# Layer-1 PV of four KV heads with V stationary, and the output projection of two of them with its weights stationary

## The chip, the cores and the metric

The kernel runs on one core of a Trainium2 chip. The metric is the device time of one execution in microseconds. Medians below are of all runs; where the fast runs alone give another size, both are given.

## The reference

One decode step of eight batch rows goes through two layers, each an attention over a cached window of 1024 positions and a feed-forward block:

```python
def _A_ref(x, k_cache, v_cache, wq, wo):       # 16 query heads, 8 KV heads (kvh), Dh = 256
    q = (x @ wq) ...
    k, v = the last W = 1024 positions, each kvh used by two query heads
    p = softmax(q k^T * Dh ** -0.5)
    return (p v) @ wo
x = x + _A_ref(_layernorm(x), k, v, wq, wo)     # layer 1, attention
x = x + _B_ref(_layernorm(x), w1, w2)           # silu feed-forward, D = 448, F = 1792
x = x + _A_ref(_layernorm(x), k, v, wq, wo)     # layer 2: the same caches and weights
x = x + _B_ref(_layernorm(x), w1, w2)
```

TensorE (PE in the profiles) does a matmul by holding one operand in its array (it is *stationary*) and streaming the columns of the other through (they *move*). PV is the product of the softmax weights p with V, wo the output projection.

Each batch row brings 8 K and 8 V tiles of 512 KB, 8.39 MB; together with the weights 77.7 MB are loaded. Both layers use the same tiles, so a tile stays in its slot until layer 2 has used it.

## The kernel before

A planner takes tasks with estimated durations and priorities, puts them in one static order per engine and inserts the semaphores. The table BIAS shifts the priorities; it was tuned for this list of tasks. PE's instructions run in that order and no other.

```python
def pv_rows(b, layer, k2, prio, oT_dst, oT_key, nj=4):   # p stationary (2 columns), V moves (256 columns)
    ...   # four KV heads side by side in four column groups of the array
    fns.append(lambda e, ...: e.matmul(bank[ob][32 * j:32 * j + 2, c0:c0 + DH], pt, vv, ...,
                                       tile_position=(0, 32 * j)))
    # then: ACT evicts the rows, two matmuls transpose them, DVE scales them into oT1

def pv_cols(b, layer, kvh, prio, oT_dst, oT_key):        # V stationary (128 columns), p moves (2 columns)
    for a in range(2):
        for u in range(8):
            fns.append(lambda e, ...: e.matmul(bank[vb][:, c0 + 2 * a:c0 + 2 * a + 2],
                                               vs[:, ...128 columns of V...], pT_sb[ei][:, u, 2 * kvh:2 * kvh + 2], ...))
    # then: DVE scales the columns into oT1, no transpose

def wo_part(b, kvhs, last, prio):                        # o stationary (1 column), wo moves (449 columns)
    ...   # 4 matmuls per kvh, accumulated as rows in bank XB

def fold(prio, scale, reads):                            # rows of XB -> columns of x in bank YB
    act(... rowb <- bank[XB] ...)                        # eviction, 0.55 us
    keep(2, prio, "part")                                # filler: 512-wide products with zero weights, results unused
    to_cols(YB, 0, rowb, ones4, 1, ...)                  # 6 matmuls: 3 of 128 columns, 2 of 64, 1 of 128

# layer 1 of batch b (cut)
pv_rows(b, 0, 0, prio, oT1, "oT1")                       # kvh 0-3
if b > 0:
    idle(4, prio, "s1", XB)                              # filler
wo_part(b, (0, 1), 7, prio + 1)
wo_part(b, (2, 3), 7, prio + 1)
pv_rows(b, 0, 1, prio, oT1, "oT1", 3)                    # kvh 4, 5, 6
wo_part(b, (4, 5, 6), 7, prio)
pv_cols(b, 0, 7, prio, oT1, "oT1")                       # kvh 7
wo_part(b, (7,), 7, prio)
fold(prio, 1.0, [])
# then layer 2 of b: feed-forward, q, scores (which free the K slots), softmax, PV (which frees the V slots)
```

Of the kernel before, what the change touches and what calls it, by code (L numbers as in the profile page):

```python
# [7 lines left out]
ALU = mybir.AluOpType  # L8
# [17 lines left out]
HOLD, PE_SCALE = 0.503, 1.091  # L26
BIAS = {"dve.KT.0.a": 11.7, "dve.KT.1.a": -6.0, "pe.S0.0.a": 9.3, "dve.mT.0.a": -6.1, "dve.mg.0.a": 26.6,
        "pe.pT.0.a": 16.5, "dve.eT.0.a": -27.1, "pe.l.0.a": 2.8, "dve.lsum.0.a": 22.2, "pe.S0.1.a": 30.5,
        "pe.pT.1.a": 11.2, "act.rsum.a": -40.4, "act..a": 25.9, "pe.PV0.0.0.a": 23.2, "pe.PV0.0.1.a": 1.7,
        "pe.PV0.0.2.a": 6.9, "pe.PV0.0.3.a": 48.5, "pe.oT.a": 7.8, "dve.oTev.a": 17.4, "pe.wo.a": 8.1,  # L30
        "pe.PV0.1.0.a": 82.1, "pe.PV0.1.1.a": 52.7, "pe.PV0.1.2.a": 74.5, "pe.PV0.1.3.a": 51.0, "pe.PVc.a":
        12.3, "pe.keep.a": 27.9, "pe.fold.a": 30.9, "dve.xb.b": 6.6, "pe.stat.b": 27.0, "pe.w1.b": 12.2,
        "pe.keep.b": -10.7, "pe.w2.b": 33.9, "pe.fold.b": 26.1, "pe.wq.b": 9.5, "pe.qturn.b": 12.2, "dve.qT2.b":
        53.5, "pe.qsel.b": 37.8, "pe.S1.0.b": 11.8, "dve.max.b": 15.5, "pe.S1.1.b": 14.2, "pe.l.c": 13.4,
        "pe.PV1.0.0.c": 11.3, "pe.PV1.0.1.c": 46.9, "pe.PV1.0.2.c": 10.7, "pe.PV1.0.3.c": 35.0, "pe.oT.c": 8.5,
        "pe.idle.a": 3.8, "pe.idle.b": 41.7}
# [220 lines left out]
def bass_interleave_layers__sliding_block_cached__dense_activation_silu__decode_kernel(  # L257
# [9 lines left out]
    P = 128  # L267
# [8 lines left out]
    XC = 5  # L276
# [73 lines left out]
    def bk(i):  # L350
        return [("bank", i)]
# [343 lines left out]
    def pv_rows(b, layer, k2, prio, oT_dst, oT_key, nj=4):  # L695
# [4 lines left out]
        for q in range(4):  # L700
            fns = []
            for u in (2 * q, 2 * q + 1):
                for j in range(nj):
                    vv = slots[slot_of[b, "v", 4 * k2 + j]][:, u * DH:u * DH + DH]
                    pt = pT_sb[ei][:, u, 8 * k2 + 2 * j:8 * k2 + 2 * j + 2]
                    fns.append(lambda e, u=u, j=j, vv=vv, pt=pt: e.matmul(  # L706
                        bank[ob][32 * j:32 * j + 2, c0:c0 + DH], pt, vv, start=(u == 0), stop=(u == 7),
                        tile_position=(0, 32 * j), skip_group_check=True))
            vr = range(4 * k2, 4 * k2 + nj)
            pe(fns, [("slot", slot_of[b, "v", g]) for g in vr] + [("pT", ei, k2)], bk(ob), (DH, 4), prio,  # L710
               "PV%d.%d.%d.%d" % (layer, b, k2, q))
# [7 lines left out]
            oT_dst[:, :, k2 * 8:k2 * 8 + 2 * nj],  # L719
            bank[lb][:, C_O + k2 * 16:C_O + k2 * 16 + 16].rearrange("p (a n) -> p a n", a=2)[:, :, 0:2 * nj],  # L720
            rl_sb[ei][:, k2 * 8:k2 * 8 + 2 * nj].unsqueeze(1).broadcast_to([P, 2, 2 * nj]), ALU.mult),
            bk(lb) + [("rl", ei, k2)], [(oT_key, 2 * h) for h in range(4 * k2, 4 * k2 + nj)], 0.18, prio, "oTev")

    def pv_cols(b, layer, kvh, prio, oT_dst, oT_key):

        ei, k2, j = layer, kvh // 4, kvh % 4
        vs = slots[slot_of[b, "v", kvh]]
        vb = LB[layer]
        c0 = C_Q + 4 * j
        fns = []  # L730
        for a in range(2):
            for u in range(8):
                fns.append(lambda e, a=a, u=u: e.matmul(
                    bank[vb][:, c0 + 2 * a:c0 + 2 * a + 2], vs[:, u * DH + a * P:u * DH + (a + 1) * P],
                    pT_sb[ei][:, u, 2 * kvh:2 * kvh + 2], start=(u == 0), stop=(u == 7)))
        pe(fns, [("slot", slot_of[b, "v", kvh]), ("pT", ei, k2)], bk(vb), (2, 1), prio, "PVc.%d" % b)
        dve(lambda e: e.tensor_tensor(
            oT_dst[:, :, 2 * kvh:2 * kvh + 2], bank[vb][:, c0:c0 + 4].rearrange("p (a n) -> p a n", a=2),
            rl_sb[ei][:, 2 * kvh:2 * kvh + 2].unsqueeze(1).broadcast_to([P, 2, 2]), ALU.mult),
            bk(vb) + [("rl", ei, k2)], [(oT_key, 2 * kvh)], 0.18, prio, "oTev")  # L740
# [23 lines left out]
    def wo_part(b, kvhs, last, prio):  # L764
# [8 lines left out]
        pe(fns, [("oT1", 2 * kvh) for kvh in kvhs] + WO_R, bk(XB) + ["part"], (D, 4), prio, "wo")  # L773
# [14 lines left out]
    def fold(prio, scale, reads):  # L788

        act(lambda e: e.activation(rowb, bank[XB][:, 0:D1], ACTF.Copy, scale=scale), bk(XB) + reads, ["rowb"], 0.6,  # L790
            prio, "rowb")
        keep(2, prio, "part")
        to_cols(YB, 0, rowb, ones4, 1, prio, ["rowb"] + ONES4, "fold", (120, 1))

    def chain(b, prio):
# [13 lines left out]
        fold(prio, rhalf[:, 0:1], ["rhalf"])  # L809
# [134 lines left out]
    def layer1(b):  # L944
# [17 lines left out]
        if b > 0:  # L962
            idle(4, prio, "s1", XB)
        wo_part(b, (0, 1), 7, prio + 1)
        wo_part(b, (2, 3), 7, prio + 1)
        pv_rows(b, 0, 1, prio, oT1, "oT1", 3)
        wo_part(b, (4, 5, 6), 7, prio)
        pv_cols(b, 0, 7, prio, oT1, "oT1")
        wo_part(b, (7,), 7, prio)
        fold(prio, 1.0, [])  # L970
# [57 lines left out]
```

## Time and profile before

| | before |
|---|---|
| time, median of 3 | 246.25 us (245.55 to 248.67) |
| PE busy | 192.4 of 247.1 us |
| DVE busy | 167.3 us |
| end of loading | about 210 us |
| mean granted clock | 0.993 |

The page cuts the span into 40 slices. In the PE row a digit is the busy share in tenths; PEclk is the granted TensorE clock in tenths of full speed, and GB/s is what the loads moved.

In the timeline, the reference mark for it is the group of 16 w1 matmuls of 448 columns, four side by side:

```profile
150.16 0.93 PE L522 MATMUL bank<-w_sb,xbt 128*1 128x448 bf16 x16
```

In the timeline, the columns are start, duration, engine, line, operation with output and inputs, and the count.

### The profile page before, as it was taken

The page shows a single profiled execution, that of the slowest core. Times are in us where ns is not written, and L with a number is a line of the kernel's source. Part 1 is how long each engine was busy: PE and PEld are TensorE (multiplying, and loading weights), DVE is VectorE, ACT ScalarE, POOL GpSimd, SP SyncE. Part 2 cuts the span into 40 slices and gives each one's busy share as a digit, 9 for nine tenths or more (in the row PEclk, how much of TensorE's full clock was granted, in tenths as well). Part 3 has the DMA queues.
Part 4 walks back from the last instruction along what each step waited for, and adds up shares of the span by engine and source line. Part 5 has one row for each costly group of instructions (what it writes and reads, how often), then busy time and mean ns, then how long its engine had stood idle before and what let it go on. Part 6 is the DMA issues. An engine that isn't in the chain of part 4 may idle for free.

```text
span 247.1 us, 8606 instructions
## 1 busy us (share of the span) xinstructions
PE 192.4 (78%) x3780; PEld 101.5 (41%) x3780; DVE 167.3 (68%) x485; ACT 89.1 (36%) x249; POOL 11.8 (5%) x25
## 2 busy tenths in 40 slices
PE   0050430379779999999999979979899999998796
PEld 0050210133345446555544645445455545444453
DVE  6549774955975888689588858956795888322322
ACT  2001172754323443253344325432534352333212
POOL 1200000000000000000000000000000000000000
PEclk9999999999999999999999999999999999999989
DMA  6999999999999998999999999999989998000000
GB/s 228 365 359 396 289 340 379 411 362 381 406 407 413 406 408 313 397 411 379 377 411 409 312 396 395 380 326 389 359 324 378 406 409 325 8 3 0 3 3 1
DMA packets 25652, 78.22 MB, mean 317 GB/s; under 512 B 2304, under 2 KB 8336, under 8 KB 25232
## 3 DMA queue, kind: packets, MB, share of 16 engines
q1 hardware_dynamic: 25616, 77.68, 83.8%
q8 instruction: 29, 0.48, 0.8%
q14 instruction: 7, 0.06, 0.1%
HBM read 77.67 MB, written 0.01 MB: 314 GB/s over the span
## 4 chain that ended last, share of the span: by engine, by line
PE 54%; SPq 21%; DMA 12%; DVE 5%; ACT 5%; issue 3%; ACTq 0%
PE bank L706 11%; DMA slot<-in_A_k_cache_dram 9%; PE bank L644 9%; SPq L485 6%; PE bank L818 6%; SPq L480 5%; SPq L442 5%; PE bank L770 4%; PE bank L777 4%; PE bank L522 2%; PE bank L805 2%; DMA slot<-in_A_v_cache_dram 2%; PE bank L784 2%; ACT qbd L676 2%; PE bank L681 2%
## 5 line engine op out<-in xcount | busy, mean ns | idle before, releaser
L953 DVE STREAM_TRANSPOSE slot<-slot 128x512 uint32<-128x512 uint32 x128 | 83.2, 686 | 7.6 <-DMA slot<-in_A_k_cache_dram 7.3
L706 PE MATMUL bank<-slot,pT_sb 128*2 128x256 bf16 x960 | 40.6, 285 | 16.3 <-DMA slot<-in_A_v_cache_dram 13.1
L644 PE MATMUL bank<-slot,qbd 128*8 128x256 bf16 x1024 | 39.2, 284 | 4.7 <-DVE slot L953 2.6
L706 PEld LDWEIGHTS bank<-slot,pT_sb 128*2 128x2 bf16 x960 | 21.5, 85 | 26.1 <-issue 19.1
L644 PEld LDWEIGHTS bank<-slot,qbd 128*8 128x8 bf16 x1024 | 22.0, 86 | 11.9 <-DVE slot L953 3.1
L676 ACT ACTIVATE qbd<-bank,mseg 128x256 bf16<-128x256 f32 x32 | 14.3, 473 | 23.1 <-DVE mseg L672 12.5
L712 ACT ACTIVATE qbd<-bank 128x256 bf16<-128x256 f32 x32 | 12.2, 382 | 24.2 <-PE bank L706 23.8
L755 POOL TENSOR_TENSOR cols_f<-cols_f 128x1 f32<-128x1 f32 x16 | 8.8, 552 | 205.3 <-ACT cols_f L753 205.3
L613 ACT ACTIVATE qbd<-bank,cols_f 128x128 bf16<-128x128 f32 x32 | 12.0, 375 | 18.2 <-PE bank L608 17.6
L777 PE MATMUL bank<-wq_sb,cols_b 128*128 128x512 bf16 x64 | 18.1, 381 | 0.0
L770 PE MATMUL bank<-wo_sb,oT 128*1 128x449 bf16 x256 | 17.8, 377 | 0.2
L718 DVE TENSOR_TENSOR oT<-bank,l_sb 128x16 bf16<-128x16 f32 (+1 forms) x32 | 6.4, 199 | 16.3 <-PE bank L714 15.7
L818 PE MATMUL bank<-wq_sb,xbt 128*1 128x512 bf16 x256 | 16.5, 378 | 0.3 <-DVE xbt L744 0.3
L784 PE MATMUL bank<-wq_sb,cols_b 128*128 128x512 bf16 x49 | 14.7, 382 | 0.0
L825 ACT ACTIVATE qrow<-bank 128x512 bf16<-128x512 f32 x16 | 9.6, 597 | 13.1 <-PE bank L818 13.1
L681 PE MATMUL bank<-qbd,swap 128*128 128x256 bf16 x32 | 7.8, 283 | 6.5 <-ACT qbd L676 6.1
L685 ACT ACTIVATE pT_sb<-bank 128x64 bf16<-128x64 f32 (+1 forms) x24 | 5.8, 241 | 19.1 <-DVE bank L684 19.1
L684 DVE STREAM_TRANSPOSE bank<-bank 128x256 f32<-128x256 f32 x24 | 10.8, 451 | 2.6 <-PE bank L681 1.4
L461 DVE TENSOR_REDUCE qbd<-wo_sb 128x5 f32<-128x2240 bf16 x4 | 9.7, 2478 | 3.6 <-DMA wo_sb<-in_A_wo_dram 3.6
L744 DVE SCALAR_TENSOR_TENSOR xbt<-bank,mask 128x5 bf16<-128x5 f32 x16 | 3.6, 226 | 9.9 <-PE bank L545 9.7
L689 DVE TENSOR_REDUCE l_sb<-bank 128x8 f32<-128x64 f32 (+1 forms) x24 | 5.7, 237 | 6.4 <-PE bank L687 6.4
L515 PE MATMUL bank<-qbd,wq_sb 128*128 128x16 bf16 x128 | 3.6, 174 | 6.9 <-DMA wq_sb<-in_A_wq_dram 6.9
(151 smaller groups left out, 237.4 us busy)
## 6 DMA issues: line engine op xcount, KB each, us to landing
slot<-in_A_k_cache_dram SPq DMA_DIRECT2D x64, 512.0 KB, 8.4
slot<-in_A_v_cache_dram SPq DMA_DIRECT2D x64, 512.0 KB, 8.2
wo_sb<-in_A_wo_dram SPq DMA_DIRECT2D x1, 3584.0 KB, 17.8
wq_sb<-in_A_wq_dram SPq DMA_DIRECT2D x3, 1024.0 KB, 6.9
w_sb<-in_B_w_dram SPq DMA_DIRECT2D x4, 336.0 KB, 16.1
w_sb<-in_B_w_dram SPq DMA_DIRECT2D x1, 1344.0 KB, 16.4
wq_sb<-in_A_wq_dram SPq DMA_DIRECT2D x2, 256.0 KB, 10.6
w_sb<-in_B_w_dram SPq DMA_DIRECT2D x4, 112.0 KB, 12.0
```

Source lines behind the costliest of these rows:

```text
L442: dma(lambda e, j=j: e.dma_start(rows[:, 3 * j:3 * j + 3, :], parts[j, 0:3 * P, :].rearrange("(c p) n -> p c n", p=P)), [("w2", j)], 3 * P ...
L480: dma(lambda e: e.dma_start(slots[s][:, :].rearrange("p (u d) -> p u d", d=DH), A_k_cache[b, kvh, S0:SK, :].rearrange("(p u) d -> p u d", ...
L485: dma(lambda e: e.dma_start(slots[s][:, :], A_v_cache[b, kvh, S0:SK, :].rearrange("(p u) d -> p (u d)", p=P)), [("slot", s)], W * DH * 2, ...
L644: fns.append(lambda e, cb=cb, par=par, j=j, kvh=kvh, kv=kv: e.matmul(bank[sc][32 * j:32 * j + 8, k2 * 256:(k2 + 1) * 256], qbd[qi][:, kvh, ...
L676: act(lambda e, k2=k2: e.activation(e_sb[ei][:, k2, :], bank[sc][:, k2 * 256:(k2 + 1) * 256], ACTF.Exp, bias=mb[ei][:, k2:k2 + 1], scale=1.0),
L681: pe([lambda e, k2=k2: e.matmul(t, swap[:, 8 - 8 * k2:8 - 8 * k2 + P], e_sb[ei][:, k2, :], start=(k2 == ks[0]), stop=(k2 == ks[-1])) for k ...
L706: fns.append(lambda e, u=u, j=j, vv=vv, pt=pt: e.matmul(bank[ob][32 * j:32 * j + 2, c0:c0 + DH], pt, vv, start=(u == 0), stop=(u == 7), ti ...
L770: fns.append(lambda e, i=i, c=c, kvh=kvh: e.matmul(bank[XB][32 * c:32 * c + 1, 0:D1], oT1[:, i % 2, i // 2:i // 2 + 1], wo_sb[:, i * DP:i ...
L777: pe([lambda e: e.matmul(bank[SC[1]][:], zero_b.broadcast_to([P, P]), wq_sb[:, 0:512], start=False, stop=True, skip_group_check=True) for ...
L784: pe(lambda e: e.matmul(bank[bi][:], zero_b.broadcast_to([P, P]), wq_sb[:, 0:512], start=False, stop=True, skip_group_check=True), [("wq", ...
L818: pe([lambda e, j=j, c=c, k2=k2, wb=wb: e.matmul(bank[wb][32 * j:32 * j + 1, :], xbt[:, xcol(c, k2):xcol(c, k2) + 1], wq_sb[:, c * HD + (( ...
L953: dve(lambda e, v=v: e.transpose(v, v), [("slot", s)], [("slot", s)], 0.67, prio, "KT.%d.%d" % (b, k // 4))
```

## The change

The layer-1 work after the last load of a batch was to become shorter. With V stationary, each KV head can be worked on alone as soon as its load has landed and the softmax of its half is done. With the wo weights stationary, the result of kvh 6 and 7 lands in the columns of x at once, so the eviction and the fold of the wo rows need not wait for them. The filler matmuls beside that fold go, and idle goes in batches 2 to 6. BIAS was tuned again.

```diff
-        if b > 0:
+        if b == 1 or b == NB - 1:
             idle(4, prio, "s1", XB)
-        wo_part(b, (0, 1), 7, prio + 1)
-        wo_part(b, (2, 3), 7, prio + 1)
-        pv_rows(b, 0, 1, prio, oT1, "oT1", 3)
-        wo_part(b, (4, 5, 6), 7, prio)
-        pv_cols(b, 0, 7, prio, oT1, "oT1")
-        wo_part(b, (7,), 7, prio)
-        fold(prio, 1.0, [])
+        wo_part(b, (0, 1), 5, prio + 1)
+        wo_part(b, (2, 3), 5, prio + 1)
+        pv_cols(b, (4, 5), LB[0], prio)
+        wo_part(b, (4, 5), 5, prio)
+        fold(prio, 1.0, [], 0)
+        pv_cols(b, (6,), OB[0], prio)
+        wo_cols(b, 6, prio)
+        pv_cols(b, (7,), LB[0], prio)
+        wo_cols(b, 7, prio)
...
+    def wo_cols(b, kvh, prio):
+        fns = []
+        for i in range(4 * kvh, 4 * kvh + 4):
+            o = oT1[:, i % 2, i // 2:i // 2 + 1]
+            for c in range(XC):                       # 3 pieces of 128 columns, 2 of 64
+                fns.append(lambda e, i=i, c=c, o=o: e.matmul(
+                    bank[YB][xpart(c), c:c + 1], xpiece(wo_sb[:, i * DP:i * DP + D], c), o, start=False, stop=True,
+                    tile_position=xpos(c), skip_group_check=True))
+            fns.append(lambda e, i=i, o=o: e.matmul(
+                bank[YB][:, XC:XC + 1], wo_sb[:, i * DP + D:i * DP + D1].broadcast_to([P, P]), o, start=False, stop=True,
+                skip_group_check=True))
...
-        keep(2, prio, "part")
+        if n:
+            keep(n, prio, "part")
```

More of the change, by code (lines that the diff above doesn't have):

```diff
@@ L25 @@
 SP_ISSUE, DMA_FIRST, DMA_LAST = 0.47, 1.2, 2.2
-HOLD, PE_SCALE = 0.503, 1.091
-BIAS = {"dve.KT.0.a": 11.7, "dve.KT.1.a": -6.0, "pe.S0.0.a": 9.3, "dve.mT.0.a": -6.1, "dve.mg.0.a": 26.6,
-        "pe.pT.0.a": 16.5, "dve.eT.0.a": -27.1, "pe.l.0.a": 2.8, "dve.lsum.0.a": 22.2, "pe.S0.1.a": 30.5,
-        "pe.pT.1.a": 11.2, "act.rsum.a": -40.4, "act..a": 25.9, "pe.PV0.0.0.a": 23.2, "pe.PV0.0.1.a": 1.7,
-        "pe.PV0.0.2.a": 6.9, "pe.PV0.0.3.a": 48.5, "pe.oT.a": 7.8, "dve.oTev.a": 17.4, "pe.wo.a": 8.1,
-        "pe.PV0.1.0.a": 82.1, "pe.PV0.1.1.a": 52.7, "pe.PV0.1.2.a": 74.5, "pe.PV0.1.3.a": 51.0, "pe.PVc.a":
-        12.3, "pe.keep.a": 27.9, "pe.fold.a": 30.9, "dve.xb.b": 6.6, "pe.stat.b": 27.0, "pe.w1.b": 12.2,
-        "pe.keep.b": -10.7, "pe.w2.b": 33.9, "pe.fold.b": 26.1, "pe.wq.b": 9.5, "pe.qturn.b": 12.2, "dve.qT2.b":
-        53.5, "pe.qsel.b": 37.8, "pe.S1.0.b": 11.8, "dve.max.b": 15.5, "pe.S1.1.b": 14.2, "pe.l.c": 13.4,
-        "pe.PV1.0.0.c": 11.3, "pe.PV1.0.1.c": 46.9, "pe.PV1.0.2.c": 10.7, "pe.PV1.0.3.c": 35.0, "pe.oT.c": 8.5,
-        "pe.idle.a": 3.8, "pe.idle.b": 41.7}
+HOLD, PE_SCALE = 0.503, 1.094
+BIAS = {"dve.KT.0.a": 22.1, "dve.KT.1.a": -3.9, "pe.pT.0.a": 6.7, "dve.eT.0.a": -25.5, "pe.S0.1.a": 7.7,
+        "pe.xinit.a": -3.8, "dve..a": 14.1, "act.rsum.a": 44.5, "pe.PV0.0.0.a": 33.7, "pe.PV0.0.2.a": -46.3,
+        "pe.PV0.0.3.a": -28.4, "act.oev.a": 45.6, "pe.wo.2.a": 44.7, "pe.wo.4.a": 39.0, "pe.fold.a": 15.8,
+        "pe.PVc.6.a": 19.1, "dve.oTev.6.a": -2.3, "pe.woc.6.a": 11.5, "pe.PVc.7.a": 15.7, "pe.woc.7.a": 14.3,
+        "dve.xb.b": 20.2, "pe.stat.b": 50.4, "pe.keep.b": -1.5, "pe.w2.b": 48.6, "act.qrow.b": 40.5,
+        "pe.qturn.b": 1.0, "pe.qsel.b": 21.7, "pe.S1.0.b": 0.2, "dve.max.b": -4.5, "pe.S1.1.b": -27.9,
+        "dve.mT.c": 18.4, "pe.pT.c": 10.4, "pe.l.c": 2.1, "dve.rl.c": -6.4, "pe.PV1.0.0.c": -1.1,
+        "pe.PV1.0.1.c": 43.4, "pe.oT.c": 24.5, "dve.oTev.c": -6.6, "pe.PV1.1.0.c": -1.9, "pe.xinit8.c": 12.6,
+        "pe.idle.e": -7.1, "dve.xbt8.e": 22.2}
 class Task:
@@ L693, in softmax, with pv_rows @@
             [(x, ei, k2) for k2 in ks for x in ("l", "rl")], 0.25 if part is None else 0.2, prio, "rl" + tag)
-    def pv_rows(b, layer, k2, prio, oT_dst, oT_key, nj=4):
+    def pv_rows(b, layer, k2, prio, oT_dst, oT_key):
         ob, lb, ei = OB[layer] if b < NB - 1 or k2 == 0 else OB[0], LB[layer], layer
@@ L702, in pv_rows @@
             for u in (2 * q, 2 * q + 1):
-                for j in range(nj):
+                for j in range(4):
                     vv = slots[slot_of[b, "v", 4 * k2 + j]][:, u * DH:u * DH + DH]
@@ L708, in pv_rows @@
                         tile_position=(0, 32 * j), skip_group_check=True))
-            vr = range(4 * k2, 4 * k2 + nj)
+            vr = range(4 * k2, 4 * k2 + 4)
             pe(fns, [("slot", slot_of[b, "v", g]) for g in vr] + [("pT", ei, k2)], bk(ob), (DH, 4), prio,
@@ L718, in pv_rows @@
         dve(lambda e: e.tensor_tensor(
-            oT_dst[:, :, k2 * 8:k2 * 8 + 2 * nj],
-            bank[lb][:, C_O + k2 * 16:C_O + k2 * 16 + 16].rearrange("p (a n) -> p a n", a=2)[:, :, 0:2 * nj],
-            rl_sb[ei][:, k2 * 8:k2 * 8 + 2 * nj].unsqueeze(1).broadcast_to([P, 2, 2 * nj]), ALU.mult),
-            bk(lb) + [("rl", ei, k2)], [(oT_key, 2 * h) for h in range(4 * k2, 4 * k2 + nj)], 0.18, prio, "oTev")
-    def pv_cols(b, layer, kvh, prio, oT_dst, oT_key):
-        ei, k2, j = layer, kvh // 4, kvh % 4
-        vs = slots[slot_of[b, "v", kvh]]
-        vb = LB[layer]
-        c0 = C_Q + 4 * j
-        fns = []
-        for a in range(2):
-            for u in range(8):
-                fns.append(lambda e, a=a, u=u: e.matmul(
-                    bank[vb][:, c0 + 2 * a:c0 + 2 * a + 2], vs[:, u * DH + a * P:u * DH + (a + 1) * P],
-                    pT_sb[ei][:, u, 2 * kvh:2 * kvh + 2], start=(u == 0), stop=(u == 7)))
-        pe(fns, [("slot", slot_of[b, "v", kvh]), ("pT", ei, k2)], bk(vb), (2, 1), prio, "PVc.%d" % b)
-        dve(lambda e: e.tensor_tensor(
-            oT_dst[:, :, 2 * kvh:2 * kvh + 2], bank[vb][:, c0:c0 + 4].rearrange("p (a n) -> p a n", a=2),
-            rl_sb[ei][:, 2 * kvh:2 * kvh + 2].unsqueeze(1).broadcast_to([P, 2, 2]), ALU.mult),
-            bk(vb) + [("rl", ei, k2)], [(oT_key, 2 * kvh)], 0.18, prio, "oTev")
@@ new lines, in pv_rows, with pv_cols @@
+            oT_dst[:, :, k2 * 8:k2 * 8 + 8],
+            bank[lb][:, C_O + k2 * 16:C_O + k2 * 16 + 16].rearrange("p (a n) -> p a n", a=2)[:, :, 0:8],
+            rl_sb[ei][:, k2 * 8:k2 * 8 + 8].unsqueeze(1).broadcast_to([P, 2, 8]), ALU.mult),
+            bk(lb) + [("rl", ei, k2)], [(oT_key, 2 * h) for h in range(4 * k2, 4 * k2 + 4)], 0.18, prio, "oTev")
+    def pv_cols(b, kvhs, vb, prio):
+        n, h0 = 2 * len(kvhs), 2 * kvhs[0]
+        c0 = C_Q + 4 * (kvhs[0] - 4)
+        for kvh in kvhs:
+            vs = slots[slot_of[b, "v", kvh]]
+            fns = []
+            for a in range(2):
+                cc = c0 + n * a + 2 * kvh - h0
+                for u in range(8):
+                    fns.append(lambda e, a=a, u=u, cc=cc, vs=vs, kvh=kvh: e.matmul(
+                        bank[vb][:, cc:cc + 2], vs[:, u * DH + a * P:u * DH + (a + 1) * P],
+                        pT_sb[0][:, u, 2 * kvh:2 * kvh + 2], start=(u == 0), stop=(u == 7)))
+            pe(fns, [("slot", slot_of[b, "v", kvh]), ("pT", 0, 1)], bk(vb), (2, 1), prio, "PVc.%d.%d" % (b, kvh))
+        dve(lambda e: e.tensor_tensor(
+            oT1[:, :, h0:h0 + n], bank[vb][:, c0:c0 + 2 * n].rearrange("p (a n) -> p a n", a=2),
+            rl_sb[0][:, h0:h0 + n].unsqueeze(1).broadcast_to([P, 2, n]), ALU.mult),
+            bk(vb) + [("rl", 0, 1)], [("oT1", 2 * kvh) for kvh in kvhs], 0.18, prio, "oTev.%d.%d" % (b, kvhs[0]))
@@ new lines, in wo_cols @@
+    def wo_cols(b, kvh, prio):
+        fns = []
+        for i in range(4 * kvh, 4 * kvh + 4):
[7 more added lines that the diff above has]
+                skip_group_check=True))
+        pe(fns, [("oT1", 2 * kvh)] + WO_R, bk(YB), (1, 1), prio, "woc.%d.%d" % (b, kvh))
@@ L772, in wo_part @@
                     start=(kvh == 0), stop=(kvh == last), tile_position=(0, 32 * c), skip_group_check=True))
-        pe(fns, [("oT1", 2 * kvh) for kvh in kvhs] + WO_R, bk(XB) + ["part"], (D, 4), prio, "wo")
+        pe(fns, [("oT1", 2 * kvh) for kvh in kvhs] + WO_R, bk(XB) + ["part"], (D, 4), prio, "wo.%d.%d" % (b, kvhs[0]))
     def keep(n, prio, after):
@@ L786, in idle, with fold @@
                [("wq", 0), "zero_b", after], bk(bi), (512, 1), prio, "idle")
-    def fold(prio, scale, reads):
+    def fold(prio, scale, reads, n):
         act(lambda e: e.activation(rowb, bank[XB][:, 0:D1], ACTF.Copy, scale=scale), bk(XB) + reads, ["rowb"], 0.6,
             prio, "rowb")
-        keep(2, prio, "part")
+        if n:
+            keep(n, prio, "part")
         to_cols(YB, 0, rowb, ones4, 1, prio, ["rowb"] + ONES4, "fold", (120, 1))
@@ L808, in chain @@
             for f in range(FC)], ["hT"] + W2_R, bk(XB) + ["part"], (D, 4), prio, "w2")
-        fold(prio, rhalf[:, 0:1], ["rhalf"])
+        fold(prio, rhalf[:, 0:1], ["rhalf"], 2)
         xcols(prio)
```

## The prediction

> **What bounds the kernel now.** I read the page first, then the queue's waits, the chain of waits and the timeline of PE over four batches. The page shows three resources close to full at once:
>
> ```profile
> PE 192.4 (78%) x3780; PEld 101.5 (41%) x3780; DVE 167.3 (68%) x485; ACT 89.1 (36%) x249; POOL 11.8 (5%) x25
> ...
> PE   0050430379779999999999979979899999998796
> ...
> GB/s 228 365 359 396 289 340 379 411 362 381 406 407 413 406 408 313 397 411 379 377 411 409 312 396 395 380 326 389 359 324 378 406 409 325 8 3 0 3 3 1
> ```
>
> Loading ends in slice 34 (34 x 247.1/40 = 210 us). Until then the rate touches 410 GB/s but falls to 312-326 about once per batch; the last 37 us are one latency chain without loads. From slice 12 on PE is "busy" nearly always, but filler matmuls (the lines named keep and idle, on zeros) are part of that.
>
> Why the dips: the load queue waits for slots. In its own waits:
>
> ```profile
> SPq L485 <- PE bank L828: 49.8, 7, 9.6
> ```
>
> That is the load of V6 of the next batch, waiting 7 us in each batch for PE to pass the layer-2 scores of the first four heads of this one (they stand just before L828 in program order). There are 30 slots and 16 tiles per batch, so V6 and V7 of batch b+1 take slots of K0-3 of batch b. Hence a **loop**: layer-2 scores of b end -> V6, V7 of b+1 are issued and land -> layer-1 PV, wo, fold -> FFN, q -> layer-2 scores of b+1. The chain shows it once outright:
>
> ```profile
> 160.14 5.84 DMA slot<-in_A_v_cache_dram
> 165.98 0.25 issue
> 166.23 1.04 PE bank L706 x24
> ```
>
> The 24 matmuls are the layer-1 PV rows of kvh 4, 5 and 6. What then lies between V6 and the end of fold, in the timeline of PE:
>
> ```profile
> 166.23 1.04 PE L706 MATMUL bank<-slot,pT_sb 128*2 128x256 bf16 x24 [1.21 <-DMA slot<-in_A_v_cache_dram]
> 167.20 0.21 PE L714 MATMUL bank<-ident,qbd 128*128 128x8 bf16 x2
> 167.27 0.38 PE L681 MATMUL bank<-qbd,swap 128*128 128x256 bf16 x2
> 167.68 0.55 PE L770 MATMUL bank<-wo_sb,oT 128*1 128x449 bf16 x8
> 168.16 0.21 PE L714 MATMUL bank<-ident,qbd 128*128 128x8 bf16 x2
> 168.30 0.55 PE L770 MATMUL bank<-wo_sb,oT 128*1 128x449 bf16 x8
> 168.78 0.56 PE L733 MATMUL bank<-pT_sb,slot 128*128 128x2 bf16 x16
> 169.27 1.04 PE L706 MATMUL bank<-slot,pT_sb 128*2 128x256 bf16 x32
> 170.14 0.93 PE L770 MATMUL bank<-wo_sb,oT 128*1 128x449 bf16 x16
> 171.00 0.60 PE L777 MATMUL bank<-wq_sb,cols_b 128*128 128x512 bf16 x2
> 171.44 0.22 PE L687 MATMUL bank<-pT_sb,cols_b 128*128 128x128 bf16 x1
> ```
>
> Fold starts at 171.91 and ends about 172.3, 6.1 us after the V6 work began. The loop in numbers: scores end 160.04; V6 in use 166.23 (6.2); fold done 172.3 (6.1); next scores end 183.62 (11.3). Sum 23.6, as measured. In the batches without that DMA wait V6 is used 4.9 us after the scores, still with little to spare. The starts of the L733 group, one per batch, lie at 122.54, 144.48, 168.78, 191.07 and 213.28: periods of 21.94, 24.30, 22.29 and 22.21, mean 22.7. The load alone would need 8.39 MB / 410 GB/s = 20.5.
>
> **What the Trainium skill says.** "TensorE: Matmul & The Clock Gate", the section on the 56 ns gap, gives a floor of about 25 ns from start to start for small matmuls. The trace agrees: 16 PV columns (L733) take 0.49 us and 4 of L828 take 0.19, so (0.49-0.19)/12 = 25 ns each plus about 0.09 on entering. "TensorEngine Tiling (Array Packing)", Key Properties, says that changing the tiling mode drains TensorE. The trace agrees: fold has three 128-wide matmuls, two 64-wide, one 128-wide:
>
> ```profile
> 154.80 0.35 PE L542 MATMUL bank<-cols_b,qrow 128*128 128x1 bf16 x5
> 155.08 0.18 PE L545 MATMUL bank<-cols_b,qrow 128*128 128x1 bf16 x1
> 155.19 0.41 PE L644 MATMUL bank<-slot,qbd 128*8 128x256 bf16 x8
> ```
>
> In narrow windows the 64-wide pair starts at 154.96, so three, two and one matmuls take 0.16, 0.12 and 0.11 us, where 25 ns each would make 0.08, 0.05 and 0.03. Each switch costs about 0.08 us. "DMA: Bandwidth & Descriptors" (Anatomy of one DMA) puts about 2 us of fixed time on a load. The trace agrees roughly: V6 takes 5.84 us, of which its own 0.52 MB at 410 GB/s are 1.3; for a us after 160 only 156 GB/s move. The first page's part on clock oscillation explains the fillers (idle PE lets its clock fall); the granted clock is 1.00 in all four periods, so the trace does not show what fewer of them do.
>
> **The change part by part**, per batch.
>
> (1) The PV rows of kvh 4-6 go: 24 matmuls, 0.76 us (163.59 to 164.35 without a wait), their ACT eviction (0.38) and their two L714 matmuls (0.14). Three column groups of 16 come: 3 x 0.49 = 1.47. They can start as soon as V4, V5 have landed, before V6 is there. PE: +0.57.
>
> (2) wo of kvh 6 and 7: 8 row matmuls go, 8 x 0.048 = 0.38 (L770 starts 0.76-0.86 apart for 16). In come 2 x 24 matmuls with weights stationary. Each of the 8 rows i is the fold pattern of 3 + 2 + 1 with two mode switches: about 0.31 us by the fold's 0.16 + 0.12 and one joining on at 25-30 ns, so 4 x 0.31 = 1.2 per kvh and 2.4 in all. Without the switches it would be 48 x 0.025 + 0.2 = 1.4. PE: +2.0.
>
> (3) rowb (ACT 0.55) and fold (PE 0.39) remain but cover kvh 0-5 only and move ahead of V6's landing, off the loop. The two keep matmuls beside them go (0.44), and in batches 2 to 6 four idle ones (4 x 0.22 = 0.88). PE: -1.32.
>
> Net on PE: +0.57 + 2.0 - 1.32 = **+1.25 us per batch** in batches 2 to 6, +2.1 in batches 1 and 7, where idle stays.
>
> On the loop: from V6, the new way is PVc.6 0.49, woc.6 1.2, PVc.7 0.49, its eviction about 0.3, woc.7 1.2 and x about 0.25: 3.9 us. V7's path alone (1.3 later, then 2.2) is shorter. So 6.1 becomes 3.9 and the loop of 23.6 would be 21.4; with V6 after 4.9 it would be 20.1, about the load's own 20.5. The loop stops binding, by up to **2.2 us per batch**.
>
> But PE's in-order stream then binds. Of the undisturbed period of 21.94 I work out some 1.0 us as waits (0.76 shown as not busy, and short ones hidden in the modelled ends of matmuls). 21.94 + 1.25 - 1.0 = 22.2 is the floor by PE if every wait is filled; the work that stood between V6 and fold (the layer-2 PV of the batch before, a softmax, wo of kvh 0-3) does not vanish, it only has to stand elsewhere. Against the mean of 22.7 that is 0.5 saved on some five periods, 2.3 us. The last batch has nothing left to overlap with: there PE's +2.1 is partly on the path, and rowb and fold (about 1.0 with their handovers) come off it: +1.0. Sum: 246.25 - 2.3 + 1.0 = **245.0 us**.
>
> **The rivals.** (a) *The loop is what counts and the extra PE work drops into waits*: period 21.2, (22.7-21.2) x 6 = 9 us less, 237 to 240. For it: the dips, the 49.8 us of queue waits, the fillers as evidence that the author had PE time to spare. Against it: PE has only 5.5 us of shown idle time from 90 to 215 us. (b) *PE becomes the bound*: no wait can be filled, the period rises to 21.94 + 1.25 or so, 23.2, and the end moves to 249 to 251. For it: PE was already at 21.2 to 21.3 busy in every period; the mode switches, which the kernel's own planner (0.0265 us per small matmul) doesn't know, so that its order is made with woc 0.5 us too short. Against it: keep and idle are real slack that was put into the stream where waits were expected. (c) *The loads were hidden anyway*: the end is set by the last batch's chain, and only its +1 or -1 us shows. Against it: the last chain cannot start before loading and the periods have passed. (d) Stalls named "issue" (1.30 at 145.90, 0.71 at 174.13), which no dependency explains: some 56 more matmuls per batch may bring more of them.
>
> **Range and chances.** Between (a) and (b) the sign is open. I put a quarter on (a), rather less on (b), the rest between: 245.0, range 240 to 250.5. Faster by over 2% means under 241.3, slower means above 251.2. Faster 0.27, same 0.57, slower 0.16. I add a little weight to faster, because the fillers were retuned for the new order.
>
> **What would show each step.** Group L733's successor with 64 matmuls per batch at 25-30 ns: step 1. The woc groups from start to the next start: 1.2 us each means that the mode switches bite, 0.7 that they don't, and then PE is 1.0 us per batch lighter and (a) gains. The queue's wait for the layer-2 scores: well below 49.8 us, with the dips gone, if the loop is shortened; unchanged if PE took its place. The distance between column groups of successive batches: 22.2, against 21.2 for (a) and 23.2 for (b). From V6's landing to the x column: 3.9. Idle time of PE outside the fillers: near none. The prediction is wrong if woc is far from 1.2, if the order puts other PE work between V7 and x again, or if the granted clock falls where fillers were dropped.

## More of the kernel before

A run counts as "fast" when it lies within 1.5% of the fastest run of its kernel.

The clock row of the kernel before is the one that the prediction did not show:

```profile
PEclk9999999999999999999999999999999999999989
```

The clock stays at the top all the time, apart from one slice near the end.

## The result

| | before | changed |
|---|---|---|
| median | 247.46 us (4 runs, 245.55 to 252.44) | 272.0 us (4 runs, 271.19 to 273.07) |
| granted clock of the runs | 0.98 to 1.00 (the runs of before beside the experiments) | 0.906 to 0.937 |

The ratio is 1.102 (95% interval 1.092 to 1.113): 10% slower. A ratio here is the mean time of one kernel's fast runs over that of the other's of the same rounds, so it is not quite the ratio of the medians quoted.

The page of the changed kernel, the rows of the slices:

```profile
PE 210.0 (78%) x4215; PEld 123.0 (46%) x4240; DVE 170.9 (63%) x493; ACT 86.0 (32%) x241; POOL 11.8 (4%) x25
...
PEclk9999999999997999599959997998699889979999
...
GB/s 246 348 408 367 312 356 409 384 370 408 353 369 272 331 364 381 261 324 327 380 217 369 290 401 255 373 344 352 232 365 345 310 290 341 160 2 2 0 2 4
```

Two things are new. The clock falls once per batch, in some slices to half. And the dips of the load rate, which the change was to remove, are deeper: 217 to 272 GB/s where before they reached 312 to 326. The load queue's waits for slots have not gone, they have moved and grown: from 98 us in all to 119. The two longest (the first, in front of the K loads, was 28.9 us before):

```profile
SPq L479 <- PE bank L764: 50.2, 6, 9.2
...
SPq L484 <- PE bank L843: 38.1, 6, 11.5
```

What stands between the softmax and the x column of one batch, in the timeline of PE (L733 is PV by columns, L784 wo by rows, L705 layer 2's PV by rows, L541 and L544 the fold, L748 and L751 the new wo columns, L764 the first use of x, L521 w1):

```profile
154.93 0.20 PE L686 MATMUL bank<-pT_sb,cols_b 128*128 128x64 bf16 x1 [0.60 <-ACT pT_sb L684]
154.96 0.55 PE L733 MATMUL bank<-pT_sb,slot 128*128 128x2 bf16 x16
...
156.47 0.95 PE L733 MATMUL bank<-pT_sb,slot 128*128 128x2 bf16 x32 [0.26 <-DVE oT L717]
157.35 1.31 PE L784 MATMUL bank<-wo_sb,oT 128*1 128x449 bf16 x24
158.59 0.56 PE L733 MATMUL bank<-pT_sb,slot 128*128 128x2 bf16 x16
159.08 0.61 PE L705 MATMUL bank<-slot,pT_sb 128*2 128x256 bf16 x16
159.62 0.35 PE L541 MATMUL bank<-cols_b,qrow 128*128 128x1 bf16 x5
159.90 0.18 PE L544 MATMUL bank<-cols_b,qrow 128*128 128x1 bf16 x1
159.94 0.34 PE L748 MATMUL bank<-oT,wo_sb 128*128 128x1 bf16 x5
160.21 0.18 PE L751 MATMUL bank<-oT,wo_sb 128*128 128x1 bf16 x1
160.25 0.34 PE L748 MATMUL bank<-oT,wo_sb 128*128 128x1 bf16 x5
...
162.48 0.71 PE L705 MATMUL bank<-slot,pT_sb 128*2 128x256 bf16 x16
163.13 0.27 PE L764 MATMUL bank<-xbt 128*128 128x1 bf16 x4
163.32 1.66 PE L521 MATMUL bank<-w_sb,xbt 128*1 128x448 bf16 x16
```

Which KV heads the three L733 groups hold is told by the evictions behind them on DVE: four columns for one head, eight for two.

```profile
156.08 0.16 DVE L737 TENSOR_TENSOR oT<-bank,l_sb 128x4 bf16<-128x4 f32 x1 [0.46 <-PE bank L713]
...
157.46 0.17 DVE L737 TENSOR_TENSOR oT<-bank,l_sb 128x8 bf16<-128x8 f32 x1 [0.74 <-PE bank L733]
...
159.75 0.12 DVE L737 TENSOR_TENSOR oT<-bank,l_sb 128x4 bf16<-128x4 f32 x1
```

So the 32 matmuls at 156.47 are kvh 4 and 5. The 16 at 154.96, in front of them, are kvh 6 and those at 158.59 kvh 7, by the static order that the program builds. From kvh 6 (154.96) to the first use of x (163.13) it takes 8.2 us. Before, the same way from the PV rows with kvh 6 (166.23) to the first use of x (172.70) took 6.5. A row of the new wo columns (six matmuls) takes 0.31 us from start to start (159.94 to 160.25), and eight of them 2.54 (159.94 to 162.48). Then the w1 group takes 1.66 us in place of 0.93: it runs at half clock. One microsecond per line, the columns being the stretch and its length, PE busy (instructions), granted clock, DMA share and GB/s:

```profile
161.00:162.00 1.00, 1.00 (x24) 1.00 1.04 426
162.00:163.00 1.00, 1.00 (x26) 0.93 0.67 258
163.00:164.00 1.00, 1.00 (x16) 0.50 0.13 53
164.00:165.00 1.00, 1.00 (x13) 0.50 0.80 225
165.00:166.00 1.00, 0.78 (x6) 0.50 0.89 348
166.00:167.00 1.00, 1.00 (x22) 0.87 1.00 381
```

PE is shown 100% busy up to the moment at which its clock is halved; the clock stays low for 3.4 us (162.85 to 166.27 in half-microsecond windows). From 64 us on, the trace has seven such dips of 3.4 or 6.8 us, 34 us in all, and each begins while the wo columns run or within 0.4 us of their end (the first two at 84.35 and 108.24). At half clock 34 us can cost at most 17.

From w1 to w1 the middle of the trace has periods of 27.1, 25.3, 26.3 and 25.9 us, against 21.9, 23.1, 22.7 and 23.0 before.

### The profile page after: what moved, and what is told of

It reads as the page before. It is cut to its first block, busy times and chain, and to the rows that moved or that the text cites. A ratio compares the mean times of both kernels' runs of the same rounds, so it can differ in the third digit from the quotient of the medians.

```text
span 269.4 us, 9505 instructions
## 1 busy us (share of the span) xinstructions
PE 210.0 (78%) x4215; PEld 123.0 (46%) x4240; DVE 170.9 (63%) x493; ACT 86.0 (32%) x241; POOL 11.8 (4%) x25
## 4 chain that ended last, share of the span: by engine, by line
PE 60%; DVE 11%; DMA 9%; SPq 8%; ACT 7%; issue 4%; DVEq 0%; ACTq 0%
PE bank L643 10%; PE bank L705 10%; DMA wo_sb<-in_A_wo_dram 7%; PE bank L748 5%; PE bank L833 5%; PE bank L521 5%; PE bank L733 5%; SPq L441 4%; PE bank L784 4%; DVE slot L968 4%; DVE qbd L460 4%; PE bank L791 3%; PE bank L751 3%; ACT qbd L612 2%; DMA slot<-in_A_v_cache_dram 2%
## 5 line engine op out<-in xcount | busy, mean ns | idle before, releaser
L705 PE MATMUL bank<-slot,pT_sb 128*2 128x256 bf16 x768 | 37.3, 301 | 10.0 <-DMA slot<-in_A_v_cache_dram 9.1
L705 PEld LDWEIGHTS bank<-slot,pT_sb 128*2 128x2 bf16 x768 | 14.9, 85 | 20.6 <-issue 12.3
L748 PE MATMUL bank<-oT,wo_sb 128*128 128x1 bf16 (+1 forms) x320 | 20.8, 178 | 1.2 <-issue 1.2
L733 PE MATMUL bank<-pT_sb,slot 128*128 128x2 bf16 x512 | 16.7, 164 | 3.6 <-DMA slot<-in_A_v_cache_dram 1.5
L733 PEld LDWEIGHTS bank<-pT_sb,slot 128*128 128x128 bf16 x512 | 14.9, 97 | 8.9 <-issue 6.2
L748 PEld LDWEIGHTS bank<-oT,wo_sb 128*128 128x128 bf16 (+1 forms) x320 | 17.6, 105 | 2.3 <-issue 1.2
L791 PE MATMUL bank<-wq_sb,cols_b 128*128 128x512 bf16 x29 | 12.2, 449 | 3.1 <-issue 2.5
L711 ACT ACTIVATE qbd<-bank 128x256 bf16<-128x256 f32 x24 | 9.1, 381 | 15.7 <-PE bank L705 15.7
L684 ACT ACTIVATE pT_sb<-bank 128x64 bf16<-128x64 f32 (+1 forms) x24 | 5.8, 240 | 25.0 <-DVE bank L683 24.9
L767 ACT ACTIVATE cols_f<-bank,cols_f 128x1 f32<-128x1 f32 x16 | 4.1, 258 | 30.1 <-PE bank L764 30.1
L521 PE MATMUL bank<-w_sb,xbt 128*1 128x448 bf16 x128 | 13.3, 566 | 0.0
```

What stands on the lines that cost most here:

```text
L521: pe([lambda e, c=c, j=j: e.matmul(bank[XB][32 * j:32 * j + 1, 0:D], xbt[:, xcol(c, j // 2):xcol(c, j // 2) + 1], w1_r(j, c), start=(c == ...
L705: fns.append(lambda e, u=u, j=j, vv=vv, pt=pt: e.matmul(bank[ob][32 * j:32 * j + 2, c0:c0 + DH], pt, vv, start=(u == 0), stop=(u == 7), ti ...
L733: fns.append(lambda e, a=a, u=u, cc=cc, vs=vs, kvh=kvh: e.matmul(bank[vb][:, cc:cc + 2], vs[:, u * DH + a * P:u * DH + (a + 1) * P], pT_sb ...
L748: fns.append(lambda e, i=i, c=c, o=o: e.matmul(bank[YB][xpart(c), c:c + 1], xpiece(wo_sb[:, i * DP:i * DP + D], c), o, start=False, stop=True,
L791: pe([lambda e: e.matmul(bank[SC[1]][:], zero_b.broadcast_to([P, P]), wq_sb[:, 0:512], start=False, stop=True, skip_group_check=True) for ...
```

## The experiments

Theory A: long runs of "thin" matmuls (one or two moving columns) count as an idle array, so that the granted clock halves behind them, for some 4 us per batch. Rival B: the clock fell because fillers were dropped. Rival C: the added PE time on the loop made it slower, the clock is a side effect. All experiments except e4 keep the static order of every engine exactly as in the kernel that they start from. Times are medians of four runs (e12: six) and clocks medians of the same runs; the kernel before had 247.5 to 247.6 us beside them, at 0.98 to 1.00.

| run | start | edit | us (range) | ratio to before (95%) | clock |
|---|---|---|---|---|---|
| e1 | changed | wo columns move 40 columns | 280.2 (277.2-281.9) | 1.123 (1.113-1.133) | 0.93 |
| e2 | changed | the same, and PV columns move 16 | 270.2 (270.1-275.2) | 1.091 (1.085-1.098) | 0.96 |
| e3 | changed | wo columns grouped by width | 266.1 (264.1-269.4) | 1.072 (1.064-1.080) | 0.91 |
| e4 | changed | fillers put back, planned anew | 286.1 (283.5-286.8) | 1.153 (1.143-1.163) | 0.92 |
| e5 | before | + 48 thin dummies per batch | 272.5 (268.1-273.6) | 1.090 (1.079-1.102) | 0.95 |
| e6 | before | + 13 wide dummies per batch | 265.5 (263.7-266.8) | 1.072 (1.065-1.079) | 0.99 |
| e7 | changed | wo columns cut to a quarter | 260.0 (255.2-262.3) | (one fast run only) | 0.92 |
| e8 | changed | e3, and 16 moving columns everywhere | 258.7 (256.6-260.5) | 1.045 (1.037-1.053) | 0.96 |
| e9 | changed | wo columns replaced by wide zero products, PV 16 | 256.8 (255.0-259.7) | 1.036 (1.026-1.045) | 0.99 |
| e10 | changed | e7, and PV 16 | 251.6 (249.2-253.8) | 1.013 (1.006-1.021) | 0.96 |
| e11 | before | the dropped fillers shrunk to one column | 248.4 (248.0-251.5) | 1.007 (0.999-1.015) | 0.98 |
| e12 | before | fold grouped by width | 248.8 (247.0-251.3) | 1.002 (0.995-1.008) | 0.99 |

The ratios are of the fast runs alone; 13 of the 50 runs in the table carry the label slow, three of them in e7. e7, e9 and e10 leave out contributions of kvh 6 and 7 on purpose. Their results still passed the comparison with the reference, which therefore is no proof of them. All the others compute the full result and were correct.

### e1: forty moving columns in the wo columns

```diff
-            o = oT1[:, i % 2, i // 2:i // 2 + 1]
+            o = oT1[:, i % 2, i // 2:i // 2 + 1].unsqueeze(1).broadcast_to([P, 8, 5])
-                    bank[YB][xpart(c), c:c + 1], xpiece(...), o, ...
+                    spread(xpart(c), c), xpiece(...), o, ...        # column c and 39 columns that nobody reads
```

> The change with one edit: each weight-stationary wo matmul moves its column 40 times (39 copies land in PSUM columns nobody reads) instead of once; the order of all engines is unchanged and a matmul of 40 columns still fits under the 25 ns from start to start. Theory A (long runs of matmuls with one or two moving columns count as an idle array, so the granted clock halves for about 4 us per batch, some 1.8 us lost x 8): clock up from 0.92-0.94 to 0.97 or more, the w1 group of 16 near 0.93 us instead of 1.66, time 256 to 263. Rival B (the clock fell because filler matmuls were dropped): clock stays below 0.95, time 270 to 274. Rival C (PE work and mode switches alone made it slow, the clock is a side effect): time within 1% of 272 although the clock is back.

A miss of the experiment itself. The added columns were not free:

```profile
162.65 0.42 PE L748 MATMUL bank<-oT,wo_sb 128*128 128x40 bf16 x5
163.00 0.21 PE L751 MATMUL bank<-oT,wo_sb 128*128 128x40 bf16 x1
163.04 0.43 PE L748 MATMUL bank<-oT,wo_sb 128*128 128x40 bf16 x5
```

A row takes 0.39 to 0.41 us now, not 0.31, which adds 0.8 us per batch to PE. The clock did not halve behind this group any more (that batch's w1 took 0.93 us; in another batch it still took 1.66), but it did halve earlier in the same batch, behind the PV columns, which still moved two columns each: the wo rows that followed took 2.42 us instead of 1.31. The verdict on A stays open here, as the two effects are mixed; 280 us was outside all expectations. The two fast runs (277.2 and 279.0) lie 6.0 us above the change by their mean, which 64 rows of 0.1 us more, 6.4 us, cover.

### e2: sixteen moving columns in the PV columns too

```diff
-                        bank[vb][:, cc:cc + 2], vs[...], pT_sb[0][:, u, 2 * kvh:2 * kvh + 2], ...
+                        bank[vb][:, cc:cc + 16], vs[...], pT_sb[0][:, u, :], ...
```

> As e1, and the V-stationary PV matmuls also move 16 columns (all heads) instead of 2, with 14 results unread. Same order, still under 25 ns each. Theory A: clock 0.99, no slice below 9 tenths after the first, time 254 to 259, at or a little under e1. Rival B: clock below 0.95, 270 to 274. Rival C: 270 to 274 with the clock back.

By the fast runs 8 us under e1 (270.2 against 278.1; ten by the medians), with the clock up from 0.93 to 0.96. The PV columns take as long as before (16 in 0.49 us) and the order is the same, so the difference goes with the clock (PE's unexplained stalls over 0.3 us are 1.1 us here and 3.0 in e1). The 0.8 us per batch of e1 are still in, which is why it stays near 270, out of A's range. It speaks against rival B: no filler was added and the clock rose.

### e3: fewer mode switches

```diff
-                fns.append(lambda e, i=i, c=c, o=o: e.matmul(
+                (fns if c < 3 else pairs).append(lambda e, i=i, c=c, o=o: e.matmul(
...
-        pe(fns, ...)
+        pe(fns + pairs, ...)
```

> The change with the 24 matmuls of each wo column group reordered: the 16 that are 128 wide first, then the 8 that are 64 wide, so two mode switches instead of eight. Still one moving column. If each switch costs about 0.08 us: a group takes 0.7 to 0.8 us instead of 1.24, 0.9 to 1.1 us per batch less on PE. Theory A: the thin run is a microsecond shorter, so the clock dips less often or less long (0.94 to 0.98), time 258 to 265. Rival B: clock unchanged at 0.92-0.94, time 264 to 268 by PE work alone. Rival C: 262 to 266 whatever the clock does.

The end of the second group of one batch and the next line (the first three matmuls of that group stand in one line of the timeline with the eight narrow ones of the first):

```profile
158.65 0.16 PE L751 MATMUL bank<-oT,wo_sb 128*128 128x1 bf16 x1
...
159.05 0.29 PE L748 MATMUL bank<-oT,wo_sb 128*64 128x1 bf16 x8
159.26 0.61 PE L705 MATMUL bank<-slot,pT_sb 128*2 128x256 bf16 x16
```

Both groups take 1.40 us (157.86 to 159.26), 0.70 each, where the change took 2.54. So the switches were 1.14 us per batch, about 0.09 each for 13 fewer of them (17 with the one into the next line, now 4), near the 0.08 that the fold had suggested. The time fell by 6 us, less than 8 x 1.14 = 9, and the clock did not recover (0.91). That speaks for C in its size and against A's hope that a shorter thin run would do.

### e4: the fillers back

```diff
-        if b == 1 or b == NB - 1:
+        if b > 0:
             idle(4, prio, "s1", XB)
...
-        fold(prio, 1.0, [], 0)
+        fold(prio, 1.0, [], 2)
```

> The change with the fillers of the kernel before put back: idle of 4 in batches 2 to 6 too, keep of 2 before the layer-1 fold. The planner places them, so the order changes a little. Rival B: clock back to 0.98 or more, time 255 to 262. Theory A: the fillers do not stand inside the thin run, clock stays below 0.96, time 268 to 278 (1.3 us more PE work per batch). Rival C: 276 to 282, as 1.3 us of work per batch is added.

With all fillers back the clock is 0.92, as without. That speaks against B as the cause of the dips, which e11 tests in a frozen order. What the 286 us are made of is not shown: this is the one run for which the planner made a new order, with a BIAS that was tuned for another list of tasks, periods went up to 32.5 us, and the fillers' own PE time is in it too.

### e5 and e6: the same time of thin and of wide matmuls in the kernel before

```diff
         to_cols(YB, 0, rowb, ones4, 1, prio, ["rowb"] + ONES4, "fold", (120, 1))
+        if scale == 1.0:
+            pl.tasks[-1].fns[:0] = dummies()
# e5: the 48 matmuls of wo_cols for rows 24 to 31, moving one column of zeros
# e6: 13 x matmul(bank[YB][:, 64:512], zeros as weights, wq_sb[:, 0:448])
```

> The kernel before, in its own order on every engine, with 48 dummy matmuls of the wo column kind (weights stationary, one moving column, of zeros, in the 3 + 2 + 1 pattern) put at the head of each layer-1 fold: about 2.5 us of PE per batch on the loop, results unchanged. To be read against e6, which adds the same time of wide matmuls in the same place. Theory A (thin runs let the granted clock halve, and that costs time): clock 0.92 to 0.96, time 276 to 284, at least 8 us above e6. Rival C (only the PE time on the loop counts): the same as e6 within 3 us. Rival B (fillers): clock stays at 0.99, all fillers are there.

> The kernel before, in its own order, with 13 dummy matmuls of 448 moving columns on zero weights at the head of each layer-1 fold, about 2.5 us per batch. Theories A and C: clock 0.99; the time rises by 7 or 8 x (2.5 less what waits absorb, up to 1 us), so 259 to 267. If the loop were not bound by PE and latency, it would stay near 250.

The wide dummies of one batch took 2.47 us (to the next start), the thin rows 0.31 each, 2.5 in all. The clock rows, e5 first (the profiled execution of e5 is one of the two of 273 us):

```profile
PEclk9999999988989599999998997999999999959979
```

```profile
PEclk9999999999979999999999999999999999999989
```

e6 answers C: 2.5 us more on the loop cost 18 us, 2.25 per batch. The loop is bound by what stands on it, almost one to one, and has hardly any slack. e5 against e6 answers A: the same place, the same order and the same duration, but thin, cost another 7 us by the medians and 4.5 by the fast runs (1.090 against 1.072, with intervals that just meet), and a clock of 0.95 instead of 0.99. That is less than A's 8 and more than C's 3, so the sign stands and the size is rough. Not all of it need be clock: e5 has four unexplained PE stalls of 0.3 to 1.0 us, 2.4 us in all, after the first batches, and e6 has none of that kind above 0.3 us.

### e7: the wo columns cut to a quarter

```diff
-        for i in range(4 * kvh, 4 * kvh + 4):
+        for i in range(4 * kvh, 4 * kvh + 1):
```

> The change in its own order, each wo column group cut from four rows to one (the result is wrong on purpose): 36 of 48 thin matmuls, about 1.9 us of PE per batch, go. Theory A: thin run too short to lower the clock, clock 0.97 or more, time 272 less 15 for work and less up to 12 for the clock: 246 to 255. Rival C: 256 to 260. If the PV columns are what lowers the clock: clock still below 0.95 and time 256 to 262.

The clock stayed at 0.92, so it is not the wo columns alone: the PV columns with two moving columns are the other half of the thin run. The time of 260 us matches the third expectation, though only one of the four runs, 255.2 us, counts as fast. In the trace three of the six dips begin at or right behind PV columns (99.76, 150.96 and 174.85) and last 10.2 us each, longer than any in the change. In the 3.4 us before each of them PE also stood idle, for 0.5 to 1.5 us.

### e8: grouped, and sixteen columns everywhere

> The change in its own order with the wo column groups as in e3 (two mode switches each) and with 16 moving columns in both the PV and the wo column matmuls, the additional products unread. Theory A: clock 0.97 or more; e3 without its clock loss, 254 to 260. Rival C: the clock is back and the time stays within 2 us of e3, 264 to 268.

The edit is that of e3 with that of e2, the wo columns moving 16 instead of 40. It is 7.4 us under e3 by the medians and 6.8 by the fast runs, with the clock at 0.96 instead of 0.91, a little below what A asked for. C's "within 2 us of e3" is refuted. Both traces have the same 4215 matmuls in the same order, so their number cannot be the reason (the unexplained stalls over 0.3 us, 2.2 us here and 3.7 in e3, may be 1.5 of it). Four slices still dip:

```profile
PEclk9999999999999999799999979997999799999999
```

### e9: the PE time of the change without the thin wo columns

```diff
-        fns = [] ... 24 thin matmuls
+        fns = [lambda e: e.matmul(bank[YB][:, 64:512], zero_b.broadcast_to([P, P]), wq_sb[:, 0:448], start=False,
+                                  stop=True, skip_group_check=True) for _ in range(kvh)]
```

> The change in its own order; the two thin wo column groups of a batch (2.5 us) replaced by 6 and 7 zero products of 448 columns, the same 2.5 us (the result is wrong on purpose: kvh 6 and 7 are missing), and PV with 16 moving columns. The PE time on the loop is that of the change, only the array is busy. Theory A': the added PE time on the loop makes about 17 of the 24.5 us and the clock the other 7: clock 0.98 or more, time 260 to 266. If the clock cost all of it: 246 to 252. If it cost nothing: 270 to 273.

The key run. In its timeline:

```profile
151.12 2.62 PE L744 MATMUL bank<-wq_sb,cols_b 128*128 128x448 bf16 x13
153.67 0.61 PE L705 MATMUL bank<-slot,pT_sb 128*2 128x256 bf16 x16
154.21 0.25 PE L756 MATMUL bank<-xbt 128*128 128x1 bf16 x4
154.39 0.93 PE L521 MATMUL bank<-w_sb,xbt 128*1 128x448 bf16 x16
```

The replaced groups take 2.55 us, as in the change, and w1 is back at 0.93. The clock:

```profile
PEclk9999999999999999999999999999999999999889
```

With the change's order and PE time, but a busy array, the kernel takes 256.8 us. So 9 of the 24.5 us come from the work and its order, and 15 go with the thin runs, within the 17 that the dips can cost at most. My expectation had been 17 and 7, so I had the shares wrong even then. Something besides the clock can be in the 15: in the changed kernel's trace PE stands still without a shown cause for 2.6 us in its three stalls over 0.5 us (0.59, 0.81 and 1.20), in e9 for 0.47. How much of that belongs to the greater number of instructions is open.

### e10: both halves of the thin run treated

> e7 (wo column groups cut to a quarter, wrong result) with PV moving 16 columns instead of 2. e7 still had a clock of 0.915 to 0.95. If the PV columns are the other half of the thin run: clock 0.98 or more and 250 to 255, 5 to 8 us under e7. If the PV width does not matter for the clock: clock below 0.95 and 257 to 262. What then remains above the kernel before is the PE time that the PV columns put on the loop.

251.6 us, 8.4 under e7 by the medians and 4.4 under its one fast run: the edit is the width of the PV columns alone, and the clock is 0.96 rather than 0.92. The clock was expected at 0.98, so the dips are fewer and not gone.

### e11: the dropped fillers, dropped alone

```diff
             idle(4, prio, "s1", XB)
+            for t in pl.tasks[-4:] if 1 < b < NB - 1 else ():
+                t.fns = [one matmul of one zero column]
```

(and the same for the layer-1 keep)

> The kernel before in its own order, where the two layer-1 keep matmuls of each batch and the four idle ones of batches 2 to 6 shrink to one moving column: the fillers that the change dropped, dropped alone. Rival B (dropped fillers let the clock fall): clock below 0.96, time 253 or more. Theory A: no long thin run, so the clock stays at 0.97 or more and the time at 244 to 250.

Same time within the interval (at most 1.5% more), clock 0.98 against 0.99 beside it. PE is busy for 8.8 us less (183.6 against 192.4) and the kernel no faster, so the fillers stood in waits. B is out as the cause of the dips: without the fillers the clock of this kernel hardly moves.

### e12: a candidate

```diff
-        fns.append(lambda e: e.matmul(bank[bank_i][:, col + XC * nb:col + (XC + 1) * nb],
+        fns.insert(3, lambda e: e.matmul(bank[bank_i][:, col + XC * nb:col + (XC + 1) * nb],
```

> A candidate: the kernel before with the six matmuls of every fold reordered, four 128 wide and then two 64 wide, as in e3. One mode switch less of about 0.08 us, twice per batch on the loop, 8 batches: 1.3 us less at most, ratio 0.994 to 1.000 to the kernel before. Not below 0.99 under any theory.

1.002 (0.995 to 1.008): no gain that could be measured. No version here beats the kernel before.

## Why the prediction was wrong

**The sizes of the operations were right.** PV columns at 25 to 30 ns each, 0.31 us for a row of wo columns, 2.5 us for both groups (predicted 2.4), the mode switch at 0.08 us (0.09 by e3). One slip of the sum changes nothing: 0.5 us saved on five periods are 2.5, not 2.3.

**The step that failed first is the loop: "So 6.1 becomes 3.9".** From the PV columns of kvh 6 to the first use of x it measured 8.2 us (154.96 to 163.13), longer than the 6.5 of before instead of shorter. The prediction took for granted that PV of kvh 4 and 5, wo of kvh 0 to 5 and the fold would "move ahead of V6's landing, off the loop". In the trace they stand behind it. In batches 0 to 6 the static order puts the PV columns of kvh 6 in front of those of kvh 4 and 5 (the new BIAS raises that group by 19.1 and has no entry for the other two). All PV columns of kvh 4 to 7 need the softmax of the second half as well, whose result PE waits for (0.60 us in front of 154.93). Then PV of kvh 6 with two small tasks and their waits, PV of kvh 4 and 5, the 24 wo rows, kvh 7, half of the layer-2 PV, the fold, both wo column groups and the rest of that PV follow one after another: 1.51 + 0.88 + 1.24 + 0.49 + 0.54 + 0.32 + 2.54 + 0.65 = 8.2. The prediction had named this ("if the order puts other PE work between V7 and x again") without giving it weight.

**The second is "21.94 + 1.25 - 1.0 = 22.2 is the floor by PE if every wait is filled".** With the clock held up (e9), the periods from w1 to w1 between 106.9 and 201.4 us are 24.0, 23.5, 23.9 and 23.2, 23.6 on average, against 22.7 before. Waits were not filled: the idle time shown in those periods is 1.4 to 1.9 us each, against 0.8 to 1.7 before. That is rival (b), "PE becomes the bound", with its period of 23.2, and its end of 249 to 251 us was 6 us short of e9's 256.8. e6 shows that work added on the loop is paid almost in full.

**The third is a term that the sum lacked.** The prediction wrote that the granted clock of 1.00 "does not show" what fewer fillers do, and kept the clock in its last sentence, tied to the fillers. The clock fell, but not for that reason (e4, e11). It fell because the PV and wo columns make a long stretch in which the array gets one or two columns per matmul. Thin against wide in the same place costs 4.5 to 7 us in the kernel before (e5, e6) and 15 in the changed one (e9), with the stalls mentioned as a possible part of both. This term alone takes the result out of the range; but e9, without it, is outside too (256.8 against 250.5), so the first two steps fail without it.

**The queue's wait** was expected "well below 49.8 us". The wait for the layer-2 scores fell to 38.1, but the one in front of the K loads grew from 28.9 to 50.2, and the dips deepened. From the issue of V6 and V7 (150.22) it is 4.7 us to PV of kvh 6, 8.2 to x and 12.0 to the next such issue (175.16), 24.9 in all where 21.4 was forecast. PE waited for the softmax and not for V6 in this batch, and between 110 and 215 us the chain holds one load (5.51 us from 123.08; before it was two, 7.03 and 5.84). So PE's order with its waits was the bound, more than the loading.

What stays open: how many columns per microsecond are needed to hold the clock (16 columns help in e2, e8 and e10 but leave dips), and what idle time adds to it. The four dips of e8 before 210 us begin at or right behind PV columns of 16, and in the 3.4 us before each of them PE also stood idle for 0.8 to 1.5 us. That suggests that idle time and narrow matmuls add up; no run tests it.

## What to carry to other kernels

Before turning a matmul round so that its weights are stationary and one or two columns move, count how long the array will be fed like that without a break, and look at the granted clock behind such a run, not at the busy share, which stays at 100%. When an operation is to be taken off a loop, check in the static order what will really stand between the last release and the end of the loop, because in-order work that "can run earlier" only does so if its own inputs are there. To separate the cost of time from the cost of kind, put the same duration of another kind in the same place, with the order frozen.

## What the Trainium skill lacked or had wrong

- "TensorE: Matmul & The Clock Gate", Part 1, says that the gate is set by "how busy the PE has been recently" and warns of idle gaps of over about 3.4 us. The halved clock of its table agrees (0.50 in the windows here). It lacks that the clock can be halved behind a run of matmuls with one or two moving columns although the trace shows PE 100% busy: it was halved at 162.85 us after some 3 us of mostly such work, and stayed low for 3.4. It also gives no width of the moving operand that holds the clock in such a run; 16 columns raised the mean clock from 0.91-0.92 to 0.96, and 448 in the wo columns with 16 in the PV columns to 0.99.
- "TensorEngine Tiling (Array Packing)", Key Properties, says that a change of tiling mode drains TensorE, without a figure. Here it is about 0.09 us per switch: 13 fewer switches in a batch saved 1.14 us of PE (e3).
- The same page, Instruction Overhead, says that a matmul with one moving column takes as long as one with 60. In rows of 128- and 64-wide pieces it did not come out so: with 40 columns a row took 0.39 to 0.41 us where one column took 0.31 (e1; the 40 results also went to scattered columns, so that width alone is the reason is not shown). In an unbroken 128-wide run 16 columns did cost nothing (16 matmuls in 0.49 us either way, e2).
